# One-piece output projection, and token AV joined with memory AV, in a recurrent-memory attention kernel

## Chip, cores and metric

The kernel runs on one core of one Trainium2 chip. The metric is the device time of one execution in microseconds (us), the median of several runs. The experiments ran on three chips. The kernel before ran again (medians 850.86, 851.10 and 850.91), the changed kernel did not; so runs are compared by their ratio to the kernel before and by their step lengths. Times in fences are microseconds from the start of the execution's span.

## The reference, cut to what matters

The sequence of 2048 rows is cut into 64 segments of 32. Each segment is attended together with 8 memory rows, and the memory rows of the output are the next segment's memory. So the 64 steps can't run in parallel. A gated MLP is mixed in; it and its preparation take the first 116 us and are not touched.

```python
for s in range(n_seg):                       # 64 steps
    h = concatenate([mem, x[:, 32*s : 32*s+32]])          # 8 + 32 rows
    q, k, v = h @ Wq, h @ Wk, h @ Wv                      # 32 heads of 128
    p = softmax(mask(q k^T * scale))
    o = (p @ v) @ Wo                                      # "AV", then the output projection
    mem = o[:, :8]                                        # needed by the next step
    outs.append(o[:, 8:])
return g * a + (1 - g) * b                                # a: all outs, b: the MLP
```

## The kernel before

One step `s` of the loop computes Q, K and V for its 32 rows, the scores, and then only the memory's share of the attention at once ("memory AV", with the normalised weights `Pm`), since the next step waits for it. The tokens' share ("token AV", weights `Px`) is done one step later, and the output projection of step `s` takes the memory rows of `s` with token rows of `s - 2`. TensorE has no slack, so independent "side work" (projections for later rows, in pieces of four matmuls of 512 columns) is placed wherever TensorE would otherwise wait for another engine: `run_fill(n)` issues `n` pieces. A bank is one of the areas of PSUM, where TensorE leaves its results; the program uses them by number, each for up to 512 columns. `wsb` is the projection's result after it was copied out of its bank, `UTT` that of the AV work. A shape like 128x32 is the part of TensorE's array that one matmul uses (rows x columns); in the shapes 128x32 and 32x128 four matmuls work side by side (in these traces four of 512 columns take 0.216 us together). Three steps of four have eight pieces; every fourth step, counted from here as "the fourth", has ten.

```python
sm = bank(nc_, ...)                                       # row sums for the memory, 128x128 array
...                                                       # 2 matmuls (L649, L650)
run_fill(5 + (si == 3))
nc.vector.reciprocal(...); Pm = E * R                     # VectorE
Um = [bank(k, [P, NG, 8]) for k in (nd, ne, na, nc_)]
av(Um, 8, s, V, Pm, 8, 0, 0)                              # memory AV: 40 matmuls, 32x128 tiles
...                                                       # token row sums into B (L660, L661), copies of Um
nc.vector.reciprocal(out=R[:, 8*NG:]..., in_=sr)          # L665
run_fill(1)
...
for half in range(2):                                     # projection, 128x32 tiles
    wp = bank((nb, nd)[half], [P, 256])
    for u in range(8):
        wo_unit(wp, UTT[Tp % 2], 24 - 8*sp, u, 256*half, 256*half + 256)
    if half == 0:
        flush(act_q, 2)
    (nc.scalar.copy if half else nc.vector.tensor_copy)(out=wsb[:, d], in_=wp[:])
...
S_next = mask_mm()                                        # L359: next scores start from the mask, 128x128
if live and s >= 1:
    av_x(s - 1, (ne, na, nc_, nb))                        # token AV: 40 matmuls, 32x128 tiles
run_fill(2 * (si == 3))
for m in range(KC):                                       # L695: 4 small matmuls transpose the new memory, 128x128
    nc.tensor.matmul(aT[:, m, :], lhsT=wsb[:, m*P:(m+1)*P], rhs=Sel[:, 0:M], ...)
nc.vector.tensor_copy(out=hn[:, :, 0:M], in_=aT)          # hT: the next step's Q waits for it
for _ in fill: pass                                       # the rest of the side work
```

## Time and profile before

| | before |
|---|---|
| time | 851.37 us median (849.81 to 851.44) |
| span, granted clock of TensorE | 848.8 us, 0.994 |
| TensorE / VectorE / ScalarE / GpSimd busy | 96 / 59 / 51 / 32% |
| first Q block of the loop, last one | 116.2 us, 822.5 us |
| step length, by place in a group of four (medians over the trace) | 11.00, 10.94, 11.04, 11.66 us |

A step length is the distance between the starts of two steps' first Q blocks on TensorE. It is so regular (most steps of one place agree within 0.01 us) that a difference of 0.02 us between two kernels can be read from it. The lines are shown with the prediction.

### The profile page before, as it was taken

The page shows a single profiled execution, that of the slowest core. Times are in us where ns is not written, and L with a number is a line of the kernel's source. Part 1 is how long each engine was busy: PE and PEld are TensorE (multiplying, and loading weights), DVE is VectorE, ACT ScalarE, POOL GpSimd, SP SyncE. Part 2 cuts the span into 40 slices and gives each one's busy share as a digit, 9 for nine tenths or more (in the row PEclk, how much of TensorE's full clock was granted, in tenths as well). Part 3 has the DMA queues.
Part 4 walks back from the last instruction along what each step waited for, and adds up shares of the span by engine and source line. Part 5 has one row for each costly group of instructions (what it writes and reads, how often), then busy time and mean ns, then how long its engine had stood idle before and what let it go on. Part 6 is the DMA issues. An engine that isn't in the chain of part 4 may idle for free.

```text
span 848.8 us, 49249 instructions
## 1 busy us (share of the span) xinstructions
PE 813.2 (96%) x22417; PEld 495.7 (58%) x22417; DVE 502.4 (59%) x1017; ACT 434.2 (51%) x1244; POOL 275.2 (32%) x625
## 2 busy tenths in 40 slices
PE   4989999999999999999999999999999999999986
PEld 2655455566656666556666665656665666656554
DVE  4555335666665666565666566666656566657553
ACT  2444454555545554555455555555454545555552
POOL 8000123333233424242424342333324342424220
PEclk8999999999999999999999999999999999999999
DMA  9890221010101010101000000101010101010000
GB/s 317 268 361 8 65 63 27 4 35 4 35 10 35 4 34 12 34 12 30 15 22 24 19 26 17 29 10 35 10 35 7 34 9 36 9 31 9 10 4 24
DMA packets 38216, 37.64 MB, mean 44 GB/s; under 512 B 13545, under 2 KB 36434, under 8 KB 36466
## 3 DMA queue, kind: packets, MB, share of 16 engines
q1 hardware_dynamic: 37874, 34.31, 12.3%
q8 instruction: 177, 2.90, 1.4%
q14 instruction: 37, 0.30, 0.1%
q0 software_dynamic: 128, 0.13, 0.1%
HBM read 26.03 MB, written 6.29 MB: 38 GB/s over the span
## 4 chain that ended last, share of the span: by engine, by line
PE 90%; DVE 6%; issue 1%; DMA 1%; SPq 1%; ACT 1%; DVEq 0%; ACTq 0%
PE b L210 34%; PE b L232 17%; PE b L221 17%; PE b L383 5%; PE hp L454 3%; PE bp L471 3%; PE b L359 2%; PE b L368 2%; PE b L660 1%; PE b L695 1%; PE b L388 1%; PE b L649 1%; DVE st L401 1%; DVE junk L422 1%; DMA Wo_sb<-in_A_x_dram 1%
## 5 line engine op out<-in xcount | busy, mean ns | idle before, releaser
L216 DVE STREAM_TRANSPOSE Tt<-b 128x512 f32<-128x512 f32 (+1 forms) x384 | 225.6, 613 | 79.1 <-PE b L210 65.4
L210 PEld LDWEIGHTS <-hT 128*32 128x32 bf16 x5120 | 134.8, 97 | 100.0 <-DVE hT L696 15.7
L232 PE MATMUL b<-Wo_sb,UTT 128*32 128x256 bf16 (+1 forms) x4736 | 162.7, 285 | 1.2 <-ACT UTT L595 0.8
L221 PE MATMUL b<-Wv_sb,hT 128*32 128x512 bf16 x2048 | 141.9, 378 | 0.0
L210 PE MATMUL b<-Wq_sb,hT 128*32 128x512 bf16 x2048 | 133.0, 379 | 1.4 <-DVE hT L696 1.4
L210 PE MATMUL b<-Wk_sb,hT 128*32 128x256 bf16 (+1 forms) x3072 | 133.4, 308 | 0.0
L232 PEld LDWEIGHTS <-UTT 128*32 128x32 bf16 x4736 | 121.3, 97 | 19.6 <-ACT UTT L595 1.5
L630 ACT CAST KT<-Tt 128x256 bf16<-128x256 f32 (+1 forms) x192 | 87.1, 476 | 53.6 <-DVE Tt L216 53.5
L581 POOL TENSOR_TENSOR Px<-E,R 128x256 bf16<-128x256 bf16 x64 | 43.1, 673 | 219.0 <-DVE R L665 219.0
L665 DVE RECIPROCAL R<-b 128x256 f32<-128x256 f32 x64 | 112.5, 1757 | 0.0
L630 POOL CAST QT<-Tt 128x512 bf16<-128x512 f32 x64 | 39.3, 614 | 192.3 <-DVE Tt L216 192.3
L595 ACT CAST UTT<-b 128x256 bf16<-128x256 f32 x256 | 76.8, 386 | 23.6 <-PE b L388 23.1
L684 ACT CAST wsb<-b 128x256 bf16<-128x256 f32 x66 | 24.6, 373 | 120.0 <-PE b L232 120.0
L653 DVE RECIPROCAL R<-b 128x64 f32<-128x64 f32 x64 | 35.6, 557 | 79.1 <-PE b L650 79.1
L630 ACT CAST QT<-Tt 128x512 bf16<-128x512 f32 x64 | 39.6, 619 | 67.6 <-DVE Tt L216 67.6
L459 ACT ACTIVATE hg<-hp,b_sb 128x256 bf16<-128x256 f32 x80 | 37.6, 473 | 54.1 <-PE hp L454 54.1
L383 PEld LDWEIGHTS <-V 32*128 32x128 bf16 x4096 | 35.2, 91 | 46.5 <-DVE Pm L655 32.4
L221 PEld LDWEIGHTS <-hT 128*32 128x32 bf16 x2048 | 49.5, 96 | 21.1
L664 ACT CAST UTT<-b 128x64 bf16<-128x64 f32 x128 | 20.9, 215 | 75.6 <-PE b L388 75.6
L454 PE MATMUL hp<-yT,w_sb 128*128 128x256 bf16 (+1 forms) x352 | 55.8, 284 | 2.5 <-DVE yT L444 2.5
L583 POOL TENSOR_TENSOR racc<-racc,R 128x320 f32<-128x320 f32 x64 | 55.6, 868 | 0.0
L471 PE MATMUL bp<-w_sb,hg 128*128 128x512 bf16 x160 | 50.0, 392 | 3.7 <-DVE c_all L474 3.7
(116 smaller groups left out, 1046.5 us busy)
## 6 DMA issues: line engine op xcount, KB each, us to landing
Wv_sb<-in_A_Wv_dram SPq DMA_DIRECT2D x4, 1024.0 KB
Wq_sb<-in_A_Wq_dram SPq DMA_DIRECT2D x4, 1024.0 KB
Wk_sb<-in_A_Wk_dram SPq DMA_DIRECT2D x4, 1024.0 KB
Wo_sb<-in_A_Wo_dram SPq DMA_DIRECT2D x2, 2048.0 KB
vd<-vt SPq DMA_DIRECT2D x32, 128.0 KB
vs<-vd SPq DMA_DIRECT2D x256, 16.0 KB
out_dram<-o SPq DMA_DIRECT2D x16, 128.0 KB
Wo_sb<-in_A_x_dram SPq DMA_DIRECT2D x1, 1024.0 KB
```

What stands on the lines that cost most here:

```text
L210: nc.tensor.matmul(bk[32 * j:32 * j + 32, 0:n], lhsT=G[:, kc, :], rhs=W5[t][:, kc, h0:h1, j, :], start=(kc == 0), stop=(kc == KC - 1), til ...
L216: nc.vector.transpose(out=Tt[:, 0:n], in_=bk[:, 0:n])
L221: nc.tensor.matmul(bk[32 * j:32 * j + 32, :], lhsT=G[:, kc, :], rhs=Wv5[:, kc, 4 * vb:4 * vb + 4, j, :], start=(kc == 0), stop=(kc == KC - ...
L232: nc.tensor.matmul(bk[32 * g:32 * g + 32, :], lhsT=ut[:, i, j, c0:c0 + 32], rhs=Wo_sb[:, 4 * i + j, d0:d1], start=(j == 0 and i < 4), stop ...
L383: nc.tensor.matmul(U[j][:, i, :], lhsT=V[q, i, :], rhs=Pt[q, i, c_main:c_main + n], start=(i == 0), stop=False, skip_group_check=True, til ...
L454: nc.tensor.matmul(hp[:rows, :], lhsT=w1_sb[:, kc, fc * P:fc * P + rows], rhs=yTs[blk][:, kc, :], start=(kc == 0), stop=(kc == KC - 1))
L471: nc.tensor.matmul(bpt[T][:], lhsT=hg_[:rows, tt * P:(tt + 1) * P], rhs=w2_sb[:rows, fc, :], start=(fc == 0), stop=(fc == FC - 1))
L581: nc.gpsimd.tensor_tensor(out=Px[:, :, 0:32], in0=E[:, :, 16:48], in1=Rr, op=ALU.mult)
L583: nc.gpsimd.tensor_tensor(out=racc[:], in0=racc[:], in1=R[:], op=ALU.add)
L595: nc.scalar.copy(out=UTT[T % 2][:, :, j, c0 + M:c0 + 40], in_=U[:])
L630: (nc.gpsimd.tensor_copy if bi == 2 else nc.scalar.copy)(out=dst, in_=Tv)
L665: nc.vector.reciprocal(out=R[:, 8 * NG:].rearrange("p (i q) -> p i q", q=32), in_=sr)
```

## The change

The intent: one wide projection in place of two halves; token AV put in front of memory AV so that it covers the wait for `Pm` and the two share four accumulator banks; and the side work that this frees spread anew, so that two pieces lie between the mask matmul and the transposing matmuls. Core of the diff (helper signatures and the last two, dead steps are cut):

```diff
-            ring = (nd, ne, na, nc_, nb)
+            ring = (nb, nd, ne, na, nc_)
...
-            run_fill(5 + (si == 3))
+            run_fill(3 + (si == 3))
...
-            Um = [bank(k, [P, NG, 8]) for k in (nd, ne, na, nc_)]
-            av(Um, 8, s, V, Pm, 8, 0, 0)
+            U4 = [bank(k, [P, NG * 40]) for k in (nd, ne, na, nc_)]
+            Um = [u[:, 0:NG * 8]... for u in U4]
+            Ux = [u[:, NG * 8:]... for u in U4]
+            if s >= 1:
+                av(Ux, 32, s - 1, Vs.pop(s - 1), Pxs.pop(s - 1), 0, 32, 24)
+                Uxs[s - 1] = Ux
+            av(Um, 8, s, V, Pm, 8, 0, 0, first=(s == 0))
...
             run_fill(1)
+            flush(act_q, 2)
...
-        for half in range(2):
-            ...
-            (nc.scalar.copy if half else nc.vector.tensor_copy)(out=wsb[:, d], in_=wp[:])
+        wp = bank(nb, [P, Dm])
+        for u in range(8):
+            wo_unit(wp, UTT[Tp % 2], 24 - 8 * sp, u)
+        nc.scalar.copy(out=wsb[:, 0:256], in_=wp[:, 0:256])
+        nc.vector.tensor_copy(out=wsb[:, 256:Dm], in_=wp[:, 256:Dm])
...
             S_next = mask_mm()
-        if live and s >= 1:
-            av_x(s - 1, (ne, na, nc_, nb))
-        run_fill(2 * (si == 3))
+        run_fill(2 + (si == 3))
```

More of the change, by code (lines that the diff above doesn't have):

```diff
@@ L375, in scores, with av @@
                                  start=False, stop=True, skip_group_check=True, tile_position=(0, 32 * j))
-    def av(U, n, s, V, Pt, c_main, c_left, u0):
+    def av(U, n, s, V, Pt, c_main, c_left, u0, first=True):
         T, si = divmod(s, SPT)
@@ L383, in av @@
                 nc.tensor.matmul(U[j][:, i, :], lhsT=V[q, i, :], rhs=Pt[q, i, c_main:c_main + n],
-                                 start=(i == 0), stop=False, skip_group_check=True, tile_position=(32 * j, 0))
+                                 start=(first and i == 0), stop=False, skip_group_check=True, tile_position=(32 * j, 0))
         for g in range(2):
@@ L584, in x_mul @@
         Pxs[s] = Px
-    def av_x(s, banks):
-        U = [bank(k, [P, NG, 32]) for k in banks]
-        av(U, 32, s, Vs.pop(s), Pxs.pop(s), 0, 32, 24)
-        Uxs[s] = U
     def ux_out(s):
@@ L594, in ux_out @@
         for j, U in enumerate(Uxs.pop(s)):
-            nc.scalar.copy(out=UTT[T % 2][:, :, j, c0 + M:c0 + 40], in_=U[:])
+            nc.scalar.copy(out=UTT[T % 2][:, :, j, c0 + M:c0 + 40], in_=U)
     for s in range(nseg + 2):
@@ L656 @@
                                     in1=R[:, 0:8 * NG].rearrange("p (i q) -> p i q", q=8).unsqueeze(2).to_broadcast([P, NG, 2, 8]), op=ALU.mult)
-            Um = [bank(k, [P, NG, 8]) for k in (nd, ne, na, nc_)]
-            av(Um, 8, s, V, Pm, 8, 0, 0)
+            U4 = [bank(k, [P, NG * 40]) for k in (nd, ne, na, nc_)]
+            Um = [u[:, 0:NG * 8].rearrange("p (i q) -> p i q", q=8) for u in U4]
+            Ux = [u[:, NG * 8:].rearrange("p (i q) -> p i q", q=32) for u in U4]
+            if s >= 1:
+                av(Ux, 32, s - 1, Vs.pop(s - 1), Pxs.pop(s - 1), 0, 32, 24)
+                Uxs[s - 1] = Ux
+            av(Um, 8, s, V, Pm, 8, 0, 0, first=(s == 0))
             sr = B[:, 0:NG * 32].rearrange("p (i q) -> p i q", q=32)
@@ L663 @@
             for j in range(4):
-                (nc.scalar.copy if j % 2 else nc.vector.tensor_copy)(out=UTT[Tp % 2][:, :, j, 24 - 8 * sp:24 - 8 * sp + M], in_=Um[j][:])
+                (nc.scalar.copy if j % 2 else nc.vector.tensor_copy)(out=UTT[Tp % 2][:, :, j, 24 - 8 * sp:24 - 8 * sp + M], in_=Um[j])
             nc.vector.reciprocal(out=R[:, 8 * NG:].rearrange("p (i q) -> p i q", q=32), in_=sr)
             run_fill(1)
+            flush(act_q, 2)
         else:
@@ L670 @@
                 x_mul(s - 1)
-                av_x(s - 1, (ne, na, nc_, 7))
+                Ux = [bank(k, [P, NG, 32]) for k in (nd, ne, na, nc_)]
+                av(Ux, 32, s - 1, Vs.pop(s - 1), Pxs.pop(s - 1), 0, 32, 24)
+                Uxs[s - 1] = Ux
             else:
@@ L676 @@
         wsb = cw.tile([P, Dm], BF16, tag="wsb", bufs=9, name="wsb")
-        for half in range(2):
-            d = slice(256 * half, 256 * half + 256)
-            wp = bank((nb, nd)[half], [P, 256])
-            for u in range(8):
-                wo_unit(wp, UTT[Tp % 2], 24 - 8 * sp, u, 256 * half, 256 * half + 256)
-            if half == 0:
-                flush(act_q, 2)
-            (nc.scalar.copy if half else nc.vector.tensor_copy)(out=wsb[:, d], in_=wp[:])
+        wp = bank(nb, [P, Dm])
[3 more added lines that the diff above has]
+        nc.vector.tensor_copy(out=wsb[:, 256:Dm], in_=wp[:, 256:Dm])
         if s >= 2:
```

## The prediction

> **What bounds the kernel now.** I read the page's busy line and its chain first, to name the engine, then the timeline of the TensorE for two steps of the loop, to see of what a step consists, then VectorE and ScalarE beside it, to see which of their results TensorE needs and how late they come. The page says:
>
> ```profile
> PE 813.2 (96%) x22417; PEld 495.7 (58%) x22417; DVE 502.4 (59%) x1017; ACT 434.2 (51%) x1244; POOL 275.2 (32%) x625
> ...
> PE 90%; DVE 6%; issue 1%; DMA 1%; SPq 1%; ACT 1%; DVEq 0%; ACTq 0%
> ...
> L232 PE MATMUL b<-Wo_sb,UTT 128*32 128x256 bf16 (+1 forms) x4736 | 162.7, 285 | 1.2 <-ACT UTT L595 0.8
> ```
>
> TensorE is busy 96% of the span and 90% of the chain that ended last; the output projection (L232) waited 1.2 us in all. There is little idle time to win. The question is what a step's length is made of. TensorE in one step (columns: start, us, engine, line, what, count):
>
> ```profile
> 412.59 0.82 PE L221 MATMUL b<-Wv_sb,hT 128*32 128x512 bf16 x12
> 413.35 0.20 PE L649 MATMUL b<-E,BO 128*128 128x64 bf16 x1
> 413.38 0.19 PE L650 MATMUL b<-E,BO 128*128 128x64 bf16 x1
> 413.51 1.05 PE L210 MATMUL b<-Wq_sb,GL 128*32 128x512 bf16 x16
> 414.38 0.39 PE L210 MATMUL b<-Wk_sb,GL 128*32 128x512 bf16 x4
> 414.75 0.36 PE L383 MATMUL b<-Pm,V 32*128 32x8 bf16 x32
> 414.96 0.23 PE L388 MATMUL b<-Pm,VL 32*128 32x32 bf16 x8
> 415.12 0.28 PE L660 MATMUL b<-E,BO 128*128 128x256 bf16 x1
> 415.24 0.19 PE L661 MATMUL b<-E,BO 128*128 128x64 bf16 x1
> 415.37 0.40 PE L210 MATMUL b<-Wk_sb,GL 128*32 128x512 bf16 x4
> 415.59 1.92 PE L232 MATMUL b<-Wo_sb,UTT 128*32 128x256 bf16 x64
> 417.45 0.36 PE L359 MATMUL b<-MkA,ident 128*128 128x448 bf16 x1
> 417.74 0.37 PE L383 MATMUL b<-Px,V 32*128 32x32 bf16 x32
> 417.96 0.24 PE L388 MATMUL b<-Px,VL 32*128 32x32 bf16 x8
> 418.13 0.26 PE L695 MATMUL b<-Sel,wsb 128*128 128x8 bf16 x4
> 418.31 0.61 PE L210 MATMUL b<-Wk_sb,GL 128*32 128x512 bf16 x8
> 418.76 0.60 PE L210 MATMUL b<-Wq_sb,hT 128*32 128x512 bf16 x8
> ```
>
> Starts, not durations, are to be read: the next group starts before the last has drained. The step before began its Q block at 407.72, so this step is 418.76 - 407.72 = 11.04 us. The Q and K blocks before this excerpt run 16 pieces of 512 columns in 0.86 us, or 53.9 ns a piece, four column tiles at once. The 12 V pieces at 412.59 should thus take 0.65 us, but the next group starts 0.76 later. The 0.11 over is found wherever the array's tile shape changes (128*32, 32*128, 128*128 in the rows): L650 takes 0.13 for 64 columns, L359 0.29 where 448 columns at the same rate are 0.19. I call this a shape change, at 0.105 us. The same step on VectorE and ScalarE:
>
> ```profile
> 413.61 0.56 DVE L653 RECIPROCAL R<-b 128x64 f32<-128x64 f32 x1 [0.87 <-PE b L650]
> 414.28 0.41 DVE L655 TENSOR_TENSOR Pm<-E,R 128x128 bf16<-128x128 bf16 x1
> 417.56 0.37 ACT L684 CAST wsb<-b 128x256 bf16<-128x256 f32 x1 [1.95 <-PE b L232]
> ```
>
> Memory AV (L383 with Pm) starts at 414.75, 0.06 after Pm ends at 414.69: in this step it just waits for it. The second projection copy begins 0.11 after L359's start and ends at 417.93, 0.20 before L695 reads it.
>
> **What the Trainium skill says.** "TensorE: Matmul & The Clock Gate", section "Back-to-back issue gap", gives columns / 2.4 + 2.5 ns per matmul. Agreed: 215.8 ns for 512 columns, and four concurrent pieces take 4 x 53.9 = 215.6 here; 256 columns give 109.2, and the 32 K pieces of 256 columns take 0.87 us, 109 per four. "TensorEngine Tiling (Array Packing)", section "Key Properties", says that changing the tiling mode, not only the tile, drains TensorE. Agreed, with the 0.105 us above, which the page doesn't give. "PSUM — Partial Sum Buffer", section "PSUM bank collisions raise a hardware error", says that two engines must not be in one bank and quadrant together, two reads included, and that the compiler back end orders any such pair. The kernel before never reads one projection bank from two engines, so its trace can't confirm it; the changed one does. The same page's "The four PSUM rules" lets a later group in a bank go without the first-matmul flag on disjoint columns: so memory AV may follow token AV in the same bank without a new start, at no cost in time.
>
> **The change part by part.**
>
> Projection: 64 pieces of 256 columns (64 x 27.3 = 1.75 us) become 32 of 512 (32 x 53.9 = 1.725). Saved: 0.025 us a step. Half the weight loads go too, but they lie under the matmuls.
>
> Shape changes: before, a step has nine (V to L649, L650 to side work, to memory AV, to L660, L661 to side work, projection to L359, to token AV, to L695, to side work). After, the two around token AV vanish, but two pieces of side work now lie between L359 and L695 and bring two back: nine again. The new pair seems 0.02 cheaper (0.10 each against 0.11). In each fourth step, where side work followed token AV even before, there were ten and will be nine: 0.105 saved.
>
> AV work: 40 + 40 matmuls before and after, 0.27 us each time; no gain.
>
> Wait for Pm: before, five side pieces (20 x 53.9 = 1.08 us) stand between L650 and memory AV, which could start 0.16 + 1.08 + 0.115 = 1.355 after L649. In the step shown Pm needs 1.40; in the step at 402.35 Pm ends at 403.28 + 0.29 = 403.57, so 1.28 with the 0.06. After, three pieces and token AV stand there: token AV starts at 0.16 + 0.65 + 0.115 = 0.92 (its fourth bank is free when the reciprocal ends, 0.82 + 0.06 = 0.88, so it doesn't wait) and ends at 1.20. Memory AV then waits 0.08 in two steps of four, and 0.20 in the third, where it waited 0.04 before. In the fourth there is a piece more (0.22) and no wait.
>
> Wait for wsb: before, L695 comes 0.68 after L359; the copy is ready at 0.11 + 0.37 + 0.06 = 0.54. After, L695 could start at 0.29 + 0.43 (two pieces) + 0.105 = 0.83. One bank is read by ScalarE, then by VectorE; if they go one after the other, 0.11 + 0.37 + about 0.05 + 0.36 + 0.06 = 0.95, and the third and fourth of the L695 matmuls need that half. They would go at about 0.87, so a wait of about 0.09 in three steps of four. In the fourth, three pieces cover it.
>
> Fourth step's tail: before, one side piece follows L695 and the next Q waited 0.13 for hT; after, two pieces follow: 0.13 saved.
>
> Sum: the two plain steps -0.045 + 0.08 + 0.09 = +0.13 each; the third -0.045 + 0.16 + 0.09 = +0.21; the fourth -0.045 - 0.105 - 0.13 = -0.28. Four steps: +0.19 us of 44.6. Over 15 such groups +2.8. In the last group there is no side work: L695 then waits for wsb from 0.68 to about 0.95, +0.26 in three or four steps, +0.9. The projections outside the 64 steps and fewer instructions to fetch give perhaps -0.3. Total +3.4: 851.4 + 3.4 = 854.8.
>
> **The rivals.** (a) The two wsb copies run together, or the order doesn't cost anything: then 3 x 0.09 x 15 = 4 us go, and the time is about 850.5. For it: nothing in the program asks for the order. Against: the page on PSUM. I give it one in five. (b) A new bound appears on VectorE: the row-sum reciprocal of 1.76 us (L665) ends 415.54 + 1.76 = 417.30, only 0.15 before L359, which overwrites its bank. If token AV or the copies push it later, L359 waits and the step grows by the shift; 0.3 us in each step would make 870. Against: it starts 0.30 after L661 in either order, and VectorE has 0.57 us idle before. One in twenty. (c) Token AV's longer life in its banks blocks the next step's Q and K. Against: ScalarE is idle before the projection's end and will copy these banks right after wsb, about 0.4 us sooner than now, so it rather helps; K and Q show no wait on banks. (d) It gains over 2%: that would need 17 us, or 0.27 a step, and the waits in a plain step are below 0.1. Only shape changes could pay this, and their number stays.
>
> **Range and chances.** Four parts in five at 854.8, one in five at 850.5, gives 854. My waits come from gaps of 0.05 to 0.1 us; 0.08 more or less in each of 64 steps is 5 us, so the range is 848 to 860. Within 2% is 834.3 to 868.4: 0.95. Slower 0.03, for rival (b); faster 0.02.
>
> **What would show it.** Right: the projection group about 1.83 us start to start, with 32 pieces; as many shape changes of 0.1; waits of TensorE for Pm (0.08 and 0.2) at the second AV; VectorE's wsb copy starting just after ScalarE's ends, and L695 spread over 0.15 us more; fourth steps shorter by 0.2 to 0.3, the others longer by 0.1 to 0.2. Wrong: VectorE's copy starting beside ScalarE's (rival a); a wait in front of L359 (rival b); plain steps shorter than 10.9 us, which would mean that a shape change costs less in the new order than I read it.

## The result, and the profile after

| | before | after |
|---|---|---|
| time, same chip | 851.4 us (849.81 to 853.06, 4 runs) | 856.91 us (856.06 to 858.06, 4 runs) |
| span, clock | 848.8 us, 0.994 | 854.3 us, 0.995 |
| first step's start; 63 steps; rest | 116.2; 706.3; 26.3 us | 116.4; 710.4; 27.5 us |
| step lengths, medians | 11.00, 10.94, 11.04, 11.66 | 11.17, 11.11, 11.28, 11.48 |

The ratio is 1.0065, with a 95% interval of 1.0042 to 1.0088. Ratios here are the mean time of one kernel's fast runs over that of the other's fast runs of the same rounds, so not quite the ratio of the medians. The kernel is 0.65% slower, inside the predicted range and inside 2%.

Of the page of the changed kernel, two lines answer to those of before:

```profile
PE 818.2 (96%) x20292; PEld 437.6 (51%) x20305; DVE 511.8 (60%) x1017; ACT 431.8 (51%) x1244; POOL 274.4 (32%) x625
...
L232 PE MATMUL b<-Wo_sb,UTT 128*32 128x512 bf16 x2624 | 161.9, 380 | 2.1 <-DVE wsb L685 1.5
```

There are 2100 fewer matmuls, and TensorE is still busy 96% of a longer span. The projection's busy time hardly moved, 162.7 to 161.9 us. So the busy line can't tell what was lost; a step's timeline can. This is the TensorE timeline of the same step of the changed kernel as the one shown of before:

```profile
409.44 1.04 PE L210 MATMUL b<-Wq_sb,hT 128*32 128x512 bf16 x16
...
415.06 0.20 PE L644 MATMUL b<-E,BO 128*128 128x64 bf16 x1
...
415.23 0.83 PE L210 MATMUL b<-Wq_sb,GL 128*32 128x512 bf16 x12
415.99 0.37 PE L383 MATMUL b<-Px,V 32*128 32x32 bf16 x32
416.20 0.24 PE L388 MATMUL b<-Px,VL 32*128 32x32 bf16 x8
416.45 0.36 PE L383 MATMUL b<-Pm,V 32*128 32x8 bf16 x32
...
417.30 1.90 PE L232 MATMUL b<-Wo_sb,UTT 128*32 128x512 bf16 x32
419.13 0.36 PE L359 MATMUL b<-MkA,ident 128*128 128x448 bf16 x1
419.42 0.61 PE L210 MATMUL b<-Wk_sb,GL 128*32 128x512 bf16 x8
419.97 0.37 PE L694 MATMUL b<-Sel,wsb 128*128 128x8 bf16 x4
420.27 0.61 PE L210 MATMUL b<-Wk_sb,GL 128*32 128x512 bf16 x8
420.71 0.82 PE L210 MATMUL b<-Wq_sb,hT 128*32 128x512 bf16 x12
```

Read starts again. The step is 420.71 - 409.44 = 11.27 us, where before it was 11.04. The projection takes 419.13 - 417.30 = 1.83, where before it took 1.86. The eight last matmuls of token AV take 416.45 - 416.20 = 0.25; without a wait they take 0.07 (the median of the fourth steps of this trace), so 0.18 of it is waiting for `Pm`. This is a third step, where the multiplication that makes `Pm` takes 0.40 us, against 0.29 in the other places; so the wait is the longest here. The four transposing matmuls (now L694) take 420.27 - 419.97 = 0.30, where L695 took 0.18 before. The two copies of `wsb` on ScalarE and VectorE are the cause of the latter:

```profile
419.25 0.37 ACT L684 CAST wsb<-b 128x256 bf16<-128x256 f32 x1 [1.93 <-PE b L232]
```

```profile
419.65 0.42 DVE L685 CAST wsb<-b 128x256 bf16<-128x256 f32 x1 [0.65 <-ACT wsb L684]
```

VectorE has been idle for 0.65 us and starts 0.03 after ScalarE's copy ends at 419.62. Nothing in the arithmetic asks for that order: both only read the bank. That both write one tile, `wsb`, isn't the reason either, by this trace: the same two engines copy `Um` out of different banks into the one tile `UTT`, and these copies start at 416.96 and 417.00 and run side by side. VectorE's copy ends at 420.07, which is 0.94 after the mask matmul's start, and the third of the transposing matmuls can't go before.

### The profile page after: what moved, and what is told of

Same layout as the page of the kernel before. It is cut to its first block, busy times and chain, and to the rows that moved or that the text cites. A ratio compares the mean times of both kernels' runs of the same rounds, so it can differ in the third digit from the quotient of the medians.

```text
span 854.3 us, 44884 instructions
## 1 busy us (share of the span) xinstructions
PE 818.2 (96%) x20292; PEld 437.6 (51%) x20305; DVE 511.8 (60%) x1017; ACT 431.8 (51%) x1244; POOL 274.4 (32%) x625
## 4 chain that ended last, share of the span: by engine, by line
PE 90%; DVE 5%; ACT 1%; issue 1%; DMA 1%; SPq 1%; POOL 0%; DVEq 0%; ACTq 0%; POOLq 0%
PE b L210 34%; PE b L232 17%; PE b L221 17%; PE b L383 4%; PE hp L454 3%; PE bp L471 3%; PE b L359 2%; PE b L694 2%; PE b L368 2%; PE b L661 1%; PE b L388 1%; PE b L644 1%; DVE st L401 1%; DVE junk L422 1%; DMA Wo_sb<-in_A_x_dram 1%
## 5 line engine op out<-in xcount | busy, mean ns | idle before, releaser
L232 PE MATMUL b<-Wo_sb,UTT 128*32 128x512 bf16 x2624 | 161.9, 380 | 2.1 <-DVE wsb L685 1.5
L232 PEld LDWEIGHTS <-UTT 128*32 128x32 bf16 x2624 | 65.2, 96 | 61.6 <-issue 4.4
L684 ACT CAST wsb<-b 128x256 bf16<-128x256 f32 x66 | 24.6, 372 | 116.4 <-PE b L232 116.4
L383 PEld LDWEIGHTS <-V 32*128 32x128 bf16 x4096 | 40.2, 91 | 31.3 <-issue 27.9
L685 DVE CAST wsb<-b 128x256 bf16<-128x256 f32 x66 | 28.0, 424 | 45.8 <-ACT wsb L684 45.8
```

Of the source, the lines that this page charges most:

```text
L232: nc.tensor.matmul(bk[32 * g:32 * g + 32, :], lhsT=ut[:, i, j, c0:c0 + 32], rhs=Wo_sb[:, 4 * i + j, d0:d1], start=(j == 0 and i < 4), stop ...
L383: nc.tensor.matmul(U[j][:, i, :], lhsT=V[q, i, :], rhs=Pt[q, i, c_main:c_main + n], start=(first and i == 0), stop=False, skip_group_check ...
```

## The experiments

Ten kernels ran. "Steps" are the four median step lengths, in the order of the tables above.

**1. The copy by ScalarE alone.** The theory is that the order of the two copies sets the time of the transposing matmuls.

```diff
-        nc.scalar.copy(out=wsb[:, 0:256], in_=wp[:, 0:256])
-        nc.vector.tensor_copy(out=wsb[:, 256:Dm], in_=wp[:, 256:Dm])
+        nc.scalar.copy(out=wsb[:], in_=wp[:])
```

> The changed kernel, with the whole projection bank (512 columns) copied out by ScalarE alone. Theory A (the two copies of one bank go one after the other, and the second one holds up the third and fourth of the four small transposing matmuls): ScalarE needs about 0.60 us for 512 columns, so wsb is ready 0.12 + 0.60 + 0.03 = 0.75 us after the mask matmul starts, before TensorE gets there at 0.84. The four matmuls take 0.19 us start to start in place of 0.30, 0.11 to 0.13 us go in three of four steps and more in the last steps without side work: 5 to 6 us less than the changed kernel, so about 851, ratio to before 1.000. Rival (the copies are not what holds up this place, or the later release of the accumulators by ScalarE costs as much): no change, ratio 1.0065.

It took 852.09 us (851.09 to 852.42), ratio to before 1.0009 (0.9996 to 1.0023). Steps 11.05, 11.00, 11.17, 11.48. On TensorE, and on ScalarE:

```profile
417.28 0.61 PE L210 MATMUL b<-Wk_sb,GL 128*32 128x512 bf16 x8
417.83 0.26 PE L693 MATMUL b<-Sel,wsb 128*128 128x8 bf16 x4
418.02 0.61 PE L210 MATMUL b<-Wk_sb,GL 128*32 128x512 bf16 x8
```

```profile
417.11 0.59 ACT L684 CAST wsb<-b 128x512 bf16<-128x512 f32 x1 [1.92 <-PE b L232]
```

The four matmuls are back at 0.19, and each of three steps lost 0.11 to 0.12; the fourth, which did not wait, lost nothing. One engine with one instruction of 0.59 us is faster than two in turn (0.82 us from ScalarE's start to VectorE's end). Theory A holds: with the turn-taking gone, most of the 0.65% is gone (ratio 1.0065 to 1.0009).

**2. Memory AV without its wait.** `Pm` of the step before is used. Its output is wrong, which doesn't matter for the time. The comparison with the reference still called the output correct, so its tolerance doesn't see this; it is an experiment all the same and not a version to keep.

```diff
-            Pm = cw.tile([P, NG, 16], BF16, tag="Pm", bufs=1, name="Pm")
+            Pm = cw.tile([P, NG, 16], BF16, tag="Pm", bufs=2, name="Pm")
...
-            av(Um, 8, s, V, Pm, 8, 0, 0, first=(s == 0))
+            av(Um, 8, s, V, Pm if s == 0 else Pm_old, 8, 0, 0, first=(s == 0))
+            Pm_old = Pm
```

> The changed kernel, wrong on purpose: memory AV reads the normalised weights Pm of the step before (two buffers), so it need not wait for this step's. Theory B (memory AV waits for Pm, because token AV and three pieces of side work cover less than five pieces did): the waits of 0.08, 0.08 and 0.20 us in three of four steps go, 5 us in all, about 852, ratio 1.001. Rival: eighty small AV matmuls in a row are held up by something else as well, as the fourth steps suggest where memory AV takes 0.05 us longer though Pm is there: then only about 2 to 3 us go, ratio 1.003 to 1.004.

It took 855.26 us (854.05 to 856.97), ratio 1.0055 (1.0040 to 1.0070): 1.7 us less than the changed kernel and not 5. Steps 11.16, 11.11, 11.16, 11.48. Only the third place gained, 0.12. The rival was right, and the timeline shows how:

```profile
415.25 0.37 PE L383 MATMUL b<-Px,V 32*128 32x32 bf16 x32
415.46 0.24 PE L388 MATMUL b<-Px,VL 32*128 32x32 bf16 x8
415.53 0.43 PE L383 MATMUL b<-Pm,V 32*128 32x8 bf16 x32
415.80 0.24 PE L388 MATMUL b<-Pm,VL 32*128 32x32 bf16 x8
```

Token AV's last eight now take 0.07, so the wait is gone. But memory AV's 32 take 0.27 where they take 0.21 after a wait (416.66 - 416.45 in the changed kernel). The single starts in the trace give the pace: up to about the 33rd of the 80 the small matmuls go in fours, one four every 25 ns (the second 39 ns after the first); from there they go one by one, 8.3 ns apart. So 80 in a row cost about 0.06 us more than 40 and 40 with a pause between, and in the first two places the wait of about 0.07 hid nearly this. "TensorE: Matmul & The Clock Gate" gives TensorE's queue a depth of 64 in its first table; 32 matmuls with their 32 weight loads would fill just that while TensorE waits, and the rest would come at the rate of issue. The count fits, and single starts within one group of 40 in the kernel before slow down at about the same number, but no run isolates it, so this cause is argued and not shown.

**3. The projection change alone.** Token AV and the side work stay as before; the projection is one piece, the banks are turned as in the changed kernel, and the side copies that were issued between the halves go in front (`flush`, cut below).

```diff
-        for half in range(2):
-            ... two banks, two copies
+        wp = bank(nb, [P, Dm])
+        ... as in the change, with both copies
...
-            av_x(s - 1, (ne, na, nc_, nb))
+            av_x(s - 1, (nd, ne, na, nc_))
```

> The kernel before with the projection in one piece of 512 columns alone: token AV stays between the mask matmul and the transposing matmuls, five pieces of side work stay before memory AV. Theory A: the transposing matmuls come 0.66 us after the mask matmul, but the second copy is ready only at 0.98, so each of three steps in four grows by about 0.3 less 0.025; the fourth has side work there and doesn't. 13 us more than before, about 864, ratio 1.015. Rival (one piece is a gain and the order of copies costs nothing): 1.6 us less than before, ratio 0.998.

It took 862.38 us (861.95 to 863.62), ratio 1.0136 (1.0119 to 1.0153). Steps 11.26, 11.19, 11.29, 11.65: 0.25 more than before in three places and 0.02 less in the fourth, where side work covers the copies. On TensorE:

```profile
422.80 0.36 PE L359 MATMUL b<-MkA,ident 128*128 128x448 bf16 x1
...
423.49 0.53 PE L694 MATMUL b<-Sel,wsb 128*128 128x8 bf16 x4
423.94 0.61 PE L210 MATMUL b<-Wk_sb,GL 128*32 128x512 bf16 x8
```

The four transposing matmuls take 0.45 in place of 0.18. So the one-piece projection is the costly part of the change, though it shortens the matmuls themselves; moving the AV work and the side work bought back about half of it.

**4. The copies in the other order**, VectorE first; one look, state unknown.

```diff
-        nc.scalar.copy(out=wsb[:, 0:256], in_=wp[:, 0:256])
-        nc.vector.tensor_copy(out=wsb[:, 256:Dm], in_=wp[:, 256:Dm])
+        nc.vector.tensor_copy(out=wsb[:, 0:256], in_=wp[:, 0:256])
+        nc.scalar.copy(out=wsb[:, 256:Dm], in_=wp[:, 256:Dm])
```

> The changed kernel with the two copies in the other order: VectorE takes the first 256 columns, ScalarE the second. In the changed kernel VectorE's copy took 0.42 us, in the kernel before 0.36. If what makes it longer is ScalarE copying at the same time (it goes on with the accumulators), VectorE takes 0.36 here; if it is GpSimd's multiplication beside it, 0.42 here too. The time stays within 2 us of the changed kernel, since the two copies still go one after the other; if they now ran side by side, it would fall by 5 us.

It took 857.71 us in its one run, with the changed kernel's step lengths. VectorE's copy again took 0.42:

```profile
419.56 0.42 DVE L684 CAST wsb<-b 128x256 bf16<-128x256 f32 x1 [0.25 <-PE b L232]
```

So ScalarE at work beside it is not what makes it longer than the 0.36 of before. GpSimd's multiplication runs beside it in both, but it isn't the cause either. The trace of the kernel before has 66 such copies: 64 follow a reciprocal without a gap and take 0.36; the last two, behind the loop, start from idle while GpSimd does nothing, and they too take 0.42. So it goes with what VectorE did just before. To follow something is not enough, though: one copy of the changed kernel, at 838.76, follows a reduction without a gap and takes 0.41.

**5 and 6. Fewer changes of the array's shape.** If a change costs 0.105 us, the mask matmul should stand beside the transposing matmuls, which use the array in the same shape. Run 5 does this to the changed kernel, run 6 adds run 1's single copy.

```diff
-        if s + 1 < nseg:
-            S_next = mask_mm()
         run_fill(2 + (si == 3))
+        if s + 1 < nseg:
+            S_next = mask_mm()
```

> The changed kernel with the mask matmul issued after the two pieces of side work, right before the small transposing matmuls (both use the whole array), so that a step has seven shape changes in place of nine. Theory C (each change of the array's tile shape costs 0.105 us, but the second copy of wsb, ready 1.00 us after where the mask matmul started, sets the end in three steps of four): those steps stay as long as they are, within 0.02 us, and the fourth, where three pieces cover, loses about 0.10 of its 0.21. About 855.5, ratio 1.005. Rival (the changes of shape add up whatever wsb does): 13 us less than the changed kernel, 844, ratio 0.991.

Run 5 took 856.24 us (855.05 to 857.07), ratio 1.0055 (1.0040 to 1.0070). Steps 11.17, 11.11, 11.28, 11.38: three places unchanged, the fourth 0.10 less. The saved changes went into the wait for VectorE's copy, which TensorE now shows openly:

```profile
420.17 0.20 PE L694 MATMUL b<-Sel,wsb 128*128 128x8 bf16 x2
420.54 0.21 PE L694 MATMUL b<-Sel,wsb 128*128 128x8 bf16 x2 [0.18 <-DVE wsb L685]
```

Two of the four matmuls go, TensorE stands idle for 0.18 us, and the other two go when VectorE's half has landed.

> The same as the run before it in this call, with wsb copied by ScalarE alone (ready at 0.75). Theory C: the three steps lose 0.08 against the changed kernel with ScalarE's copy alone (they then wait for wsb from 0.62 to 0.76), the fourth 0.22, together about 7 us less than its 852: 845, ratio 0.993. Rival (a shape change hides in waits anyway and costs nothing by itself): 852, ratio 1.001.

Run 6 took 845.22 us (844.10 to 845.68), ratio 0.9926 (0.9911 to 0.9940). Steps 10.98, 10.91, 11.08, 11.26: against run 1 each of three places lost 0.08 (they now wait for the copy: their transposing matmuls come 0.33 after the mask matmul, those of the fourth 0.20) and the fourth 0.22, for two changes of shape. On TensorE the mask matmul follows side work and the transposing matmuls follow the mask:

```profile
414.62 0.60 PE L210 MATMUL b<-Wk_sb,GL 128*32 128x512 bf16 x8
415.16 0.36 PE L359 MATMUL b<-MkA,ident 128*128 128x448 bf16 x1
415.49 0.26 PE L693 MATMUL b<-Sel,wsb 128*128 128x8 bf16 x4
```

Theory C holds in both: a change of shape costs 0.11 us where nothing else is being waited for, and nothing where something is.

**7 and 8. The same idea on the kernel before.** The mask matmul goes behind token AV; in the fourth steps two pieces of side work (run 7) or one (run 8) go in front of token AV.

```diff
-        if s + 1 < nseg:
-            S_next = mask_mm()
+        run_fill(2 * (si == 3))                # run 8: 1 * (si == 3)
         if live and s >= 1:
             av_x(s - 1, (ne, na, nc_, nb))
-        run_fill(2 * (si == 3))
+        if s + 1 < nseg:
+            S_next = mask_mm()
```

> The kernel before (projection in two pieces, token AV after the projection) with the mask matmul moved behind token AV, next to the small transposing matmuls, and in the fourth steps the two pieces of side work moved in front of token AV, next to the projection: one shape change less in three steps, two less in the fourth. Theory C: the transposing matmuls come 0.57 us after where the mask matmul started, and wsb is ready at 0.54, so nothing waits: 0.11 less in three steps, about 0.22 in the fourth, 8 to 9 us less than before: 842.5, ratio 0.990. Rival (no gain from fewer shape changes): 851, ratio 1.000.

Run 7 took 850.64 us (849.79 to 851.22), ratio 0.9992 (0.9978 to 1.0006): my expectation failed. Steps 11.06, 10.99, 11.08, 11.45: the fourth gained its 0.21, the others lost 0.05. The reason is in two rows, on TensorE and on VectorE:

```profile
416.89 0.54 PE L383 MATMUL b<-Px,V 32*128 32x32 bf16 x32
417.27 0.23 PE L388 MATMUL b<-Px,VL 32*128 32x32 bf16 x8
```

```profile
414.98 1.76 DVE L665 RECIPROCAL R<-b 128x256 f32<-128x256 f32 x1
416.66 0.36 DVE L684 CAST wsb<-b 128x256 bf16<-128x256 f32 x1
```

Token AV's 32 take 0.38 in place of 0.21. Its fourth accumulator is `nb`, the bank of the projection's first half, and VectorE copies that half only after its 1.76 us reciprocal, until 417.02, though the half was ready long before. The mask matmul used to stand in front and hid this. No row names this wait (the groups merge it), but the single starts show it: three of the 32 go at 416.89, and the fourth, the first that writes to `nb`, at 417.07, 0.05 after the copy has ended. A test of its own follows below.

> The same as the run before it in this call, but in the fourth steps one piece of side work in front of token AV and two after the transposing matmuls, so that the next Q doesn't wait 0.13 us for the new memory columns. By theory C 2 us less than that run, about 840.5, ratio 0.9875. Rival (that wait only moves to another place in the step): no difference between the two.

Run 8 took 849.15 us (848.60 to 850.68), ratio 0.9978 (0.9962 to 0.9994). Steps 11.05, 10.99, 11.08, 11.32: the fourth 0.13 less than in run 7, as expected, and 1.5 us in the time; its level was off by the same miss as run 7's.

**9 and 10. The copies' engines exchanged**: ScalarE, which is idle then, takes the first half. Run 9 is run 8 with this, run 10 the kernel before with this alone.

```diff
-            (nc.scalar.copy if half else nc.vector.tensor_copy)(out=wsb[:, d], in_=wp[:])
+            (nc.vector.tensor_copy if half else nc.scalar.copy)(out=wsb[:, d], in_=wp[:])
```

> The kernel before with the mask matmul late and one piece of side work ahead of token AV in the fourth steps, as in the last run of the second call, and with the two projection copies' engines exchanged: ScalarE copies the first half, VectorE the second. In that run token AV took 0.38 us for its first 32 matmuls in place of 0.21: theory D is that its fourth accumulator lies in the bank of the first half, which VectorE copies only after its 1.76 us reciprocal, 0.17 after token AV could start. ScalarE is free earlier, so the wait goes: 0.17 in three steps of four and about 0.1 in the fourth, 8 to 9 us, 841, ratio 0.988. Rival (token AV is slow there because it starts right behind the projection, with its weights not yet loaded, or for some other reason of TensorE itself): 849, ratio 0.998.

Run 9 took 841.25 us (840.77 to 841.88), ratio 0.9888 (0.9873 to 0.9903). Steps 10.89, 10.83, 10.92, 11.32: 0.16 less than run 8 in three places, though nothing in the fourth, where I had expected 0.1: there token AV's 32 took 0.21 in run 8 already, behind the piece of side work, so there was no wait to lose. Token AV is back at 0.21, and the mask and transposing matmuls follow at once:

```profile
414.23 0.37 PE L383 MATMUL b<-Px,V 32*128 32x32 bf16 x32
414.44 0.24 PE L388 MATMUL b<-Px,VL 32*128 32x32 bf16 x8
414.61 0.36 PE L359 MATMUL b<-MkA,ident 128*128 128x448 bf16 x1
414.81 0.24 PE L695 MATMUL b<-Sel,wsb 128*128 128x8 bf16 x4
```

> Control for the run before it in this call: the kernel before with nothing but the two engines exchanged. Theory D: no change, since token AV there comes 0.30 us later, after the mask matmul, and VectorE's second half is ready at 0.12 + 0.42 + 0.03 = 0.57 us, before the transposing matmuls at 0.68: ratio 0.999 to 1.001. If the exchange itself is worth something, for example by freeing VectorE, about 1 per cent less.

Run 10 took 849.83 us (849.31 to 852.75), ratio 0.9989 (0.9975 to 1.0003): the same. So the exchange is worth nothing by itself and 8 us once the mask matmul no longer hides the late bank. Theory D holds. Run 9 beats the kernel before by 1.1% and the changed one by 1.8% (841.25 against 856.91).

## Why the prediction was right, point by point

The predicted time was 854.0 with 848 to 860; 856.9 was measured. Against the steps of its sum:

| place in four | predicted | measured |
|---|---|---|
| first | +0.13 | +0.16 |
| second | +0.13 | +0.17 |
| third | +0.21 | +0.24 |
| fourth | -0.28 | -0.19 |
| sum | +0.19 | +0.39 (from unrounded medians) |

- **Projection, -0.025.** Right: 1.83 us start to start was forecast and seen. Run 3 shows the same 0.02 in its fourth place.
- **Shape changes.** Right in number (nine and nine, ten and nine) and in price: runs 6 and 9 give 0.11 each. The 0.02 that the new pair was to save did not come: its two changes take about 0.11 and 0.12, those of the old pair 0.11 and 0.10 (start to start, less the matmuls' own time).
- **Wait for `Pm`, 0.08, 0.08, 0.20, 0.** The wait was there in this size: 0.07, 0.07, 0.18, 0. But the prediction took AV work as 0.27 us each whether joined or not; run 2 shows that the two joined cost 0.06 more when they are not interrupted. In the first two places this and the wait overlap; in the fourth it came on top.
- **Wait for `wsb`, 0.09.** The mechanism was right, the size low: run 1 measured 0.11 to 0.12. The term was VectorE's copy, put at the 0.36 of before; it takes 0.42 here.
- **Fourth step, -0.28.** It was -0.19. The extra 0.06 of the joined AV work is more than half of the gap, and the 0.02 of the new pair another part.
- **Last group and ends, +0.6 together.** The three last steps without side work grew by 0.6 in all (10.80, 10.74, 10.86 to 11.03, 10.99, 10.99), where I had put 0.9. But the part behind the last step's start grew by 1.2, where I had put -0.3. The last two projections now share one bank and wait for the copies of the one before: the projection's row of the changed kernel, above, has 1.5 us of waiting for VectorE's `wsb`, and there were none such before (in all, the row's waiting grew from 1.2 to 2.1 us).
- **What the sum leaves over.** Fifteen groups of four at +0.39 are 5.8 us and the three steps 0.6, but the 63 steps together grew by 4.1 only. The largest part of the rest is the second step, 12.52 before and 11.11 after, and the prediction did not see it. It is no accident of one trace: the six kernels with five pieces in front of memory AV (before, runs 3 and 7 to 10) have 12.4 to 14.1 there, the six with three have 10.9 to 11.1. In the six with five, a transposition of side work stands before the reciprocal for `Pm` in VectorE's queue, and the reciprocal starts 1.93 us after the second row-sum matmul; in the others it is 0.23. So the change gains about 1.4 us there. Other odd long steps, up to 0.9 us above their place's median, stand at much the same places in kernels of one kind; I didn't study them.
- **Luck.** The steps and the ends were to cost 3.4 us and measured 5.8 + 0.6 + 1.2 = 7.6. That the total was 5.5 is mostly due to the second step, which was not forecast. The mechanisms were right; that the total came so close is in part luck.
- **Rivals.** (a), the copies side by side, is refuted by VectorE's 0.65 us of idleness ended by ScalarE's copy. (b), a wait in front of the mask matmul for the reciprocal, did not come: the reciprocal ends at 417.25 + 1.76 = 419.01, still 0.12 ahead. (c) showed nothing. (d) would have needed fewer changes of shape; that this is where the gain lies, runs 6 and 9 confirm.

So the change fails to pay because the piece that looked like the gain, one wide projection, lets a single bank be copied only by one engine after the other, on the path from one step's memory to the next. The rest of the change hides most of that, and adds a wait of its own.

## What to carry to other kernels

On a saturated TensorE, look at start-to-start distances against the ideal stream: the losses here were changes of array shape at 0.11 us each, so put matmuls of one shape next to each other before shaving columns. Two engines that emptied one PSUM bank took turns here; one instruction on one engine was then faster (0.59 against 0.82 us), and two engines worked side by side only out of different banks (the copies of `Um`). A matmul that seems to cost something may be hiding a late bank behind it, so when removing it pays nothing, look for which release became the new wait.

## What the Trainium skill lacked or had wrong

- "TensorEngine Tiling (Array Packing)", "Key Properties", says that a mode switch drains TensorE and gives no price. The runs: 0.105 to 0.11 us for each change among 128x32, 32x128 and 128x128, nine of them in a step of 11 us; nothing where TensorE has to wait anyway (run 5).
- "PSUM — Partial Sum Buffer", "PSUM bank collisions raise a hardware error", tells of the ordering of two engines' reads, and the trace agrees: the second engine started 0.03 to 0.04 us after the first one's end, in either order (runs 3 and 4 too). That section doesn't say what this costs: here 0.82 us for 256 + 256 columns in turn, against 0.59 for 512 by ScalarE alone.
- "TensorE: Matmul & The Clock Gate", "Wait — 56ns, not 53.3ns?", has start-to-start never below about 25 ns, however few the columns. Small matmuls in four row tiles went in fours here, one four every 25 ns, so the floor seems to hold for each set of four tiles. The page lacks that in a long row of them they go one by one, 8.3 ns apart, after about the 33rd (run 2).
- No page gives a number for what the instruction before it changes in a VectorE copy out of PSUM: 256 columns took 0.42 us from idle, with GpSimd at work (run 4) or at rest (the last two copies of the kernel before), and 0.36 right behind a reciprocal (its other 64).
